# An attention and two feed-forward layers on one core: inverse sums per pair of heads, early signs on other engines, and a re-timed plan

## The chip, the cores and the metric

One core of a Trainium2 chip runs the whole program in one launch. The metric is the device time in microseconds (us) of one execution, as a median over runs; less is better. Engines are called PE (TensorE, matmuls), PEld (its weight loads), DVE (VectorE), ACT (ScalarE), POOL (GpSimd) and SP (SyncE, which issues the transfers).

## The reference

```python
def _attn_ref(q, k, v, proj):            # q, k, v: (2, 8, 768, 64); proj: (64, 6)
    q_bits = (einsum('bhsd,dk->bhsk', q, proj) > 0)
    k_bits = (einsum('bhsd,dk->bhsk', k, proj) > 0)
    mask = q_bucket[:, :, :, None] == k_bucket[:, :, None, :]   # buckets: the 6 bits as a number
    scores = where(mask, q @ k.T / 8, -1e9)
    attn = exp(scores - max(scores))
    attn = attn / (sum(attn) + 1e-09)
    return attn @ v

x = attn_out as (1536, 512)
h = x @ w_in;  x = (h * sigmoid(h)) @ w_out            # 512 -> 2048 -> 512
a, b = x @ w1, x @ w2                                  # 512 -> 1024 each
out = ((a * b) @ w3) @ w_out2                          # 1024 -> 1024 -> 512
```

All of it is float32. There are 16 heads, worked on as 8 pairs.

## The kernel before, in words

**Order of the work.** Nothing is written in the order in which it runs. The kernel hands many small operations to a planner (`Plan`), each with the engines that may run it and a length in ns for each, the operations that it waits for, the buffers that it takes and gives back, and a due time. `Plan.run` (L184) plays the program: it goes through the engines again and again, takes the one that can start earliest, and there the ready operation with the earliest due time, whose instructions it writes at once. The result is one fixed list per engine, and on the chip each engine works through its list in order: an instruction that waits holds up all behind it. Due times are shifted by a table `OFF` (L43 on) with one number per name of operation and stage of the program (`shift`, L112). So a length or a number of that table moves instructions between places and, where an operation may run on two engines, between engines. Lengths cost no time on the chip.

**Attention.** Per pair of heads q, k and the two heads' V are loaded (`fetch`, `fetch_v`), the hash bits are projected (L584) and compared (L590), and per head there are six units of 128 queries. A unit is one score pass on PE (L717; mask bits ride along as extra rows), the row maximum on DVE (`peak`, L733), the exponent on ACT (`exp`, L739, which also adds up its row sums), and a transposition of 32x32 blocks on DVE (`swap`, L757). Scores have two PSUM buffers, exponents two in SBUF. When all twelve units of a pair are transposed, six weighing passes on PE multiply them with V (`weigh`, L775), and ACT and DVE move the results out (`move`, L794 and L796). Pair 0 is `lone`: one score pass (L729) fills both buffers, for both heads of the pair.

V has one buffer. The next pair's V is loaded when the last weighing pass of the pair before has read it; two copies (`double`, a helper whose lines are L320 on ACT and L324 on POOL) put it on the upper 64 partitions too.

**Inverse sums.** For each head the sums [128 x 6] get a constant added (L804) and are inverted (L805) on DVE, turned on PE (`flip`, L808), copied to SBUF by ACT (`unload`), sent to DRAM by a transfer (`send`) and read back onto 64 partitions (`spread`); `norm` multiplies the pair's result with them.

**Weights.** They arrive as 64-bit words, 512 KB at a time, in half blocks of 512 columns, and become float32 in `piece`: ACT takes the high word (`high`, L366), ACT or POOL the low word (`low`, L370 or L374), DVE joins them (`join`, L380) and the sign is put in: in early weights (needed before 60.5 us: w_out2 and the first block of w3) by DVE (`sign`, L385), in those after it by ACT and POOL (`side`, L391, and `signed`, L394). Then a high and a low part for PE are made of each (`hi`, `lo`).

**Combine passes.** w3 and w_out2 are multiplied into one matrix beforehand (`product`, L852): 8 blocks of 8 groups of three matmuls of 512 columns, 192 in all, laid between the attention's passes. The block `it` may start when the weighing of a given pair is done.

**Feed-forward.** After the attention PE works through the two layers (L1014, L1132, L1176), 1920 matmuls of 512 columns; a few of them (blocks called early, and those on the first 512 tokens) already stand among pair 7's passes. Two token blocks are folded: sums and differences of them are made and split by ACT and DVE (`split_pair`), and seven products give what eight would (`rise_pair`, L1014).

## Time and profile before

| | |
|---|---|
| median of 3 runs | 730.82 us (730.27 to 735.04) |
| the profiled execution, its own time | 735.71 us |
| its span, first to last instruction | 733.9 us |
| busy: PE, DVE, ACT, POOL | 686.0, 566.3, 379.7, 288.2 us |
| mean granted clock of PE | 0.963 of full speed |

How to read it: the span is what the profile shows, the 1.8 us around it are start and end. Busy shares are means over stages that have different limits, so the rows below go by stretches. A granted clock of 1.00 is 2.4 GHz and 0.50 is 1.2 GHz; a mean between them says for how much of a stretch either was granted.

### The profile page before, as it was taken

The page shows a single profiled execution, that of the slowest core. Times are in us where ns is not written, and L with a number is a line of the kernel's source. Part 1 is how long each engine was busy: PE and PEld are TensorE (multiplying, and loading weights), DVE is VectorE, ACT ScalarE, POOL GpSimd, SP SyncE. Part 2 cuts the span into 40 slices and gives each one's busy share as a digit, 9 for nine tenths or more (in the row PEclk, how much of TensorE's full clock was granted, in tenths as well). Part 3 has the DMA queues.
Part 4 walks back from the last instruction along what each step waited for, and adds up shares of the span by engine and source line. Part 5 has one row for each costly group of instructions (what it writes and reads, how often), then busy time and mean ns, then how long its engine had stood idle before and what let it go on. Part 6 is the DMA issues. An engine that isn't in the chain of part 4 may idle for free.

```text
span 733.9 us, 14436 instructions
## 1 busy us (share of the span) xinstructions
PE 686.0 (93%) x5800; PEld 555.3 (76%) x5800; DVE 566.3 (77%) x829; ACT 379.7 (52%) x700; POOL 288.2 (39%) x274
## 2 busy tenths in 40 slices
PE   7877879989979898799999999999999999999997
PEld 5656667767757677687788888888888888888876
DVE  5888858877878799599899897977898826938255
ACT  4655747666674767555755454343554635323030
POOL 3744976885867732344124213022263220210000
PEclk8779699999998999999999999999999999999999
DMA  7534646455555432501231411112010211100004
GB/s 213 162 113 110 185 126 179 114 180 136 159 142 155 130 117 73 185 1 58 87 95 49 144 57 44 44 58 87 29 57 15 82 63 50 50 1 1 0 1 171
DMA packets 22882, 68.34 MB, mean 93 GB/s; under 512 B 3872, under 2 KB 4640, under 8 KB 22304
## 3 DMA queue, kind: packets, MB, share of 16 engines
q1 hardware_dynamic: 22816, 67.43, 30.3%
q8 instruction: 45, 0.74, 0.4%
q14 instruction: 21, 0.17, 0.1%
HBM read 55.58 MB, written 5.29 MB: 83 GB/s over the span
## 4 chain that ended last, share of the span: by engine, by line
PE 71%; DVE 9%; DMA 8%; ACT 6%; issue 4%; POOL 2%; SPq 0%; ACTq 0%; POOLq 0%; DVEq 0%
PE more L1176 18%; PE more L1014 13%; PE more L1132 6%; PE acc L1176 6%; PE acc L775 6%; PE score L717 6%; PE acc L1014 5%; PE acc L1132 4%; DMA V<-in_v 4%; ACT P L739 2%; PE turn L775 2%; PE score L729 2%; DMA raw<-in_w 2%; DVE y L327 1%; DMA raw<-in_wo 1%
## 5 line engine op out<-in xcount | busy, mean ns | idle before, releaser
L1014 PE MATMUL more<-y,piece 128*128 128x512 f32 x462 | 111.5, 390 | 1.6 <-ACT sg L320 0.7
L757 DVE STREAM_TRANSPOSE pt<-P 128x768 f32<-128x768 f32 x96 | 91.6, 966 | 20.9 <-ACT P L739 20.8
L739 ACT ACTIVATE P<-score,st 128x768 f32<-128x768 f32 x96 | 85.9, 896 | 40.2 <-DVE st L733 35.0
L733 DVE TENSOR_REDUCE st<-score 128x1 f32<-128x770 f32 x96 | 89.0, 944 | 22.1 <-PE score L717 16.6
L1014 PEld LDWEIGHTS more<-y,piece 128*128 128x128 f32 x462 | 86.4, 188 | 20.8 <-ACT sg L320 1.1
L1176 PE MATMUL more<-gh,piece 128*128 128x512 f32 x284 | 96.4, 389 | 0.0
L775 PE MATMUL turn<-pt,V 32*64 32x193 f32 x1536 | 77.2, 340 | 4.5 <-issue 4.3
L775 PE MATMUL acc<-pt,V 32*64 32x193 f32 x1536 | 77.4, 340 | 3.0 <-DVE x L1079 2.0
L1195 DVE SCALAR_TENSOR_TENSOR X<-more,X 128x512 f32<-128x512 f32 x93 | 62.6, 682 | 14.7 <-PE more L1176 14.5
L717 PE MATMUL score<-ka,qa 128*128 128x384 f32 x168 | 51.6, 390 | 23.3 <-ACT P L739 12.7
L775 PEld LDWEIGHTS acc<-pt,V 32*64 32x64 f32 x1536 | 60.7, 136 | 10.6 <-issue 6.6
L775 PEld LDWEIGHTS turn<-pt,V 32*64 32x64 f32 x1536 | 58.2, 136 | 7.9 <-issue 7.3
L1176 PEld LDWEIGHTS more<-gh,piece 128*128 128x128 f32 x284 | 53.2, 188 | 11.2 <-DVE piece L327 0.2
L717 PEld LDWEIGHTS score<-ka,qa 128*128 128x128 f32 x168 | 29.1, 202 | 42.2 <-ACT P L739 20.3
L1132 PE MATMUL more<-x,piece 128*128 128x512 f32 x240 | 59.1, 389 | 0.0
L1176 PE MATMUL more<-gl,piece 128*128 128x512 f32 x142 | 55.3, 389 | 0.0
L852 PE MATMUL acc<-piece,piece 128*128 128x512 f32 x192 | 52.1, 409 | 0.7 <-ACT X L794 0.7
L1132 PEld LDWEIGHTS more<-x,piece 128*128 128x128 f32 x240 | 45.0, 188 | 9.4
L374 POOL TENSOR_SCALAR t<-raw 128x512 uint32<-128x512 uint32 x22 | 15.7, 714 | 79.9 <-DMA raw<-in_wo 38.0
L717 PE MATMUL score<-kb,qb 76*128 76x384 f32 x168 | 45.6, 354 | 0.0
L1176 PE MATMUL more<-piece,gh 128*128 128x512 f32 x144 | 44.4, 389 | 0.0
L1014 PE MATMUL acc<-y,piece 128*128 128x512 f32 x168 | 43.1, 391 | 0.3 <-ACT sg L320 0.3
(192 smaller groups left out, 1461.0 us busy)
## 6 DMA issues: line engine op xcount, KB each, us to landing
raw<-in_w SPq DMA_DIRECT2D x24, 512.0 KB
raw<-in_wo SPq DMA_DIRECT2D x21, 512.0 KB
raw<-in_win SPq DMA_DIRECT2D x13, 512.0 KB
...
```

The lines of the kernel that those rows point to most:

```text
L374: engine[e].tensor_scalar(out=plan[t], in0=pair(raw)[:, :, 0], scalar1=0.875 * 2.0 ** -29, scalar2=0.49, op0=ALU.mult, op1=ALU.add,)
L717: nc.tensor.matmul(out=sc[:, g, :HF], lhsT=lhs[:k, qs], rhs=rhs[:k, g * HF:g * HF + HF], start=(k == 128), stop=(k != 128),)
L729: nc.tensor.matmul(out=plan["S", "u", side * NQ + i][:, g, :HF], lhsT=lhs[k, qs], rhs=rhs[k, g * HF:g * HF + HF], start=(p == 0), stop=(p ...
L733: nc.vector.tensor_reduce(out=plan[uk("st")][:, 0:1], in_=plan[uk("S")][:, :, :HF + 1], op=ALU.max, axis=AX.XY, negate=True)
L739: nc.scalar.activation(out=plan[uk("P")], in_=plan[uk("S")][:, :, :HF], func=AF.Exp, bias=s[:, 0:1], accum_out=plan[hk("sums")][:, i:i + 1],)
L757: nc.vector.transpose(plan[mine][:, :, 32 * i:32 * i + 32], plan[uk("P")].rearrange("p g (b i) -> p (g b) i", i=32))
L775: nc.tensor.matmul(out=to[a][64 * side:64 * side + 64, :GW + 1], lhsT=V[rows_, c, side], rhs=plan[key(f"pt{side}")][rows_, c, :GW + 1], st ...
L852: nc.tensor.matmul(out=plan[key + ("ps",)], lhsT=w[:, a, k], rhs=r[:, c], start=(k == 0 and n == 0), stop=(k == 7 and n == 2),)
L1014: nc.tensor.matmul(out=plan[bk[b]], lhsT=w[:, a], rhs=y, start=(opens and j == 0 and m == 0), stop=(j == 1 and m == 2), skip_group_check=True)
L1132: nc.tensor.matmul(out=plan[key], lhsT=w[:, a], rhs=x, start=(k == 0 and n == 0), stop=(k == 3 and n == 2))
L1176: nc.tensor.matmul(out=plan[key], lhsT=a, rhs=x, start=(f == 0 and n == 0), stop=(f == 1 and n == 2))
L1195: nc.vector.scalar_tensor_tensor(out=dst, in0=plan[key], scalar=by, in1=dst, op0=ALU.mult, op1=ALU.add)
```

## The change

- **Inverse sums per pair.** Both heads of a pair write their sums into one [128 x 12] tile. It is turned as it is, ACT adds the constant while it copies the [12 x 128] result to SBUF, DVE inverts it there in place, and one send carries both heads. The add on DVE and the per-head steps are gone.
- **Signs.** `by_pool` now holds for the early weights too.
- **Lengths.** The planner counts 1200 ns instead of 390 on top of a `lone` score pass, 80 ns more on each other score pass and 100 ns more on each weighing pass. An operation without instructions, `settled`, makes it take V as there 3 us after its loads have ended in its play.
- **Table.** Every number of `OFF` is another.

```diff
 OFF = {
-    "add": (0.0, 0.0, 78.9, -161.2, -8.9),
+    "add": (0.0, 0.0, -12.7, -284.8, 10.05),
...
-                by_pool = BEGIN + 50 < need and beside
+                by_pool = beside
...
+        settled = op({"": 3000.0}, lambda e: None, loadv[:2], t0)
...
-            loadv.append(op({"POOL": 1467, "ACT": 1510}, double, loadv[:2], t0 + 4 + f))
+            loadv.append(op({"POOL": 1467, "ACT": 1510}, double, [settled], t0 + 4 + f))
...
-                        accum_out=plan[hk("sums")][:, i:i + 1],
+                        accum_out=plan[key("sums")][:, par * NQ + i:par * NQ + i + 1],
...
-                    sc = both[i] = op({"PE": 390 + 8 * (PE_MORE + HF * PE_COL) if lone else 4 * (PE_MORE + HF * PE_COL)},
+                    sc = both[i] = op({"PE": 1200 + 8 * (PE_MORE + HF * PE_COL) if lone else 80 + 4 * (PE_MORE + HF * PE_COL)},
...
-                    xo = op({"PE": 180 + 2 * PART * (18 + 2 * (GW + 1) * PE_COL)}, weigh, [*evicted[0], *evicted[1], *loadv[2:], xo],
+                    xo = op({"PE": 280 + 2 * PART * (18 + 2 * (GW + 1) * PE_COL)}, weigh, [*evicted[0], *evicted[1], *loadv[2:], xo],
...
-            def invert(e, hk=hk):
-                s = plan[hk("sums")]
-                nc.vector.tensor_scalar_add(s[:, :NQ], s[:, :NQ], (S + 1e-9) * FLOOR)
-                nc.vector.reciprocal(out=s[:, NQ:], in_=s[:, :NQ])
...
-            iv = op({"DVE": 1020}, invert, exps, te + 3)
-            fl = op({"PE": 110}, flip, [iv], te + 4, [("R", hk("it"))], [hk("sums")])
-            un = op({"ACT": act(128)}, unload, [fl], te + 4.5, [("wsb", hk("invt"))], [hk("it")])
...
+            if par == 1:
+
+                def flip(e, key=key):
+                    nc.tensor.transpose(plan[key("it")][:2 * NQ, :128], plan[key("sums")], ident)
+
+                def unload(e, key=key):
+                    nc.scalar.activation(out=plan[key("invt")][:2 * NQ, :128], in_=plan[key("it")][:2 * NQ, :128], func=AF.Copy,
+                                         bias=(S + 1e-9) * FLOOR)
+
+                def invert(e, key=key):
+                    x = plan[key("invt")][:2 * NQ, :128]
+                    nc.vector.reciprocal(out=x, in_=x)
+
+                fl = op({"PE": 110}, flip, pair_exps, te + 3, [("R", key("it"))], [key("sums")])
+                un = op({"ACT": act(128)}, unload, [fl], te + 3.5, [("wsb", key("invt"))], [key("it")])
+                iv = op({"DVE": 850}, invert, [un], te + 4)
```

Three places of the new lists. First PE, where the first combine passes stand (L852 before, L857 now; `ka_113` and `ka_114` are the two heads' buffers). Before:

```order
L717 MATMUL score_80<-ka_114,qa_110 128x384 x2
L717 MATMUL score_80<-kb_116,qb_112 128x384 x2
L717 MATMUL score_79<-ka_113,qa_109 128x384 x2
L717 MATMUL score_79<-kb_115,qb_111 128x384 x2
L852 MATMUL acc_81<-piece_83,piece_87 128x512 x3
L717 MATMUL score_80<-ka_113,qa_109 128x384 x2
L717 MATMUL score_80<-kb_115,qb_111 128x384 x2
L852 MATMUL acc_81<-piece_83,piece_87 128x512 x3
L852 MATMUL acc_81<-piece_84,piece_87 128x512 x6
```

Now, on the same engine:

```order
L717 MATMUL score_80<-ka_114,qa_110 128x384 x2
L717 MATMUL score_80<-kb_116,qb_112 128x384 x2
L584 MATMUL turn_77<-qraw_103,pt 32x384 x2
L584 MATMUL turn_77<-kraw_104,pt 32x384 x2
L857 MATMUL acc_82<-piece_83,piece_87 128x512 x6
L857 MATMUL acc_82<-piece_84,piece_87 128x512 x6
L857 MATMUL acc_82<-piece_85,piece_87 128x512 x6
L717 MATMUL score_79<-ka_114,qa_110 128x384 x2
L717 MATMUL score_79<-kb_116,qb_112 128x384 x2
L857 MATMUL acc_82<-piece_86,piece_87 128x512 x3
```

Before, the first group stands behind the first scores of pair 2 (its first head, `ka_113`), one group at a time; now six groups in a row stand behind the tenth of its twelve score passes (second head, `ka_114`). Counted by pair, from its first score pass to the next pair's, the 64 groups stood as 16, 12, 15, 13 and 8 in pairs 2 to 6 and stand now as 10, 15, 13, 16 and 10.

Second DVE, where pair 0 ends and pair 1 begins (`P_117` and `P_118` are the exponents' buffers; `pt_125` and `pt_126` are pair 0's swapped tiles, `pt_127` is pair 1's first; L590 is the comparison of hash bits). Before:

```order
L733 TENSOR_REDUCE st_122<-score_80 128x1
L590 TENSOR_SCALAR bits_108<-turn_78,sel 128x384
L804 TENSOR_SCALAR sums_123<-sums_123 128x6
L805 RECIPROCAL sums_123<-sums_123 128x6
L733 TENSOR_REDUCE st_119<-score_79 128x1
L380 SCALAR_TENSOR_TENSOR acc_81<-acc_81,t_95 128x512
L733 TENSOR_REDUCE st_120<-score_80 128x1
L804 TENSOR_SCALAR sums_124<-sums_124 128x6
L805 RECIPROCAL sums_124<-sums_124 128x6
L385 SCALAR_TENSOR_TENSOR x_93<-raw_91,acc_81 128x512
L757 STREAM_TRANSPOSE pt_125<-P_117 128x24x32
L380 SCALAR_TENSOR_TENSOR acc_82<-acc_82,t_94 128x512
```

Now, on the same engine (L813 is the new reciprocal):

```order
L733 TENSOR_REDUCE st_122<-score_80 128x1
L380 SCALAR_TENSOR_TENSOR t_95<-acc_81,t_95 128x512
L757 STREAM_TRANSPOSE pt_125<-P_117 128x24x32
L757 STREAM_TRANSPOSE pt_126<-P_118 128x24x32
L733 TENSOR_REDUCE st_119<-score_79 128x1
L733 TENSOR_REDUCE st_120<-score_80 128x1
L813 RECIPROCAL wsb_96<-wsb_96 12x128
L757 STREAM_TRANSPOSE pt_127<-P_117 128x24x32
L733 TENSOR_REDUCE st_121<-score_79 128x1
```

The last swaps of pair 0 stood behind the first two maxima of pair 1 and both inversions; now they stand ahead of them, and the one reciprocal of the pair comes behind.

Third ACT, from the moves of a pair's weighed results to the copy of the next pair's V (`fv` is the move's added column, `wsb` the unloaded sums). Before:

```order
L794 ACTIVATE X<-acc_81,fv_106 128x6x32
L366 ACTIVATE acc_81<-raw_91 128x512
L320 ACTIVATE wsb_96<-turn_78 6x128
L739 ACTIVATE P_117,sums_124<-score_79,st_121 128x768
L366 ACTIVATE acc_81<-raw_90 128x512
L739 ACTIVATE P_118,sums_124<-score_80,st_122 128x768
L391 ACTIVATE x_93<-raw_91 128x512
L320 ACTIVATE wsb_96<-turn_78 6x128
L320 ACTIVATE V_105<-V_105 64x1536
```

Now, on the same engine:

```order
L794 ACTIVATE X<-acc_81,fv_106 128x6x32
L366 ACTIVATE acc_81<-raw_91 128x512
L739 ACTIVATE P_117,sums_123<-score_79,st_119 128x768
L366 ACTIVATE acc_81<-raw_90 128x512
L739 ACTIVATE P_118,sums_123<-score_80,st_120 128x768
L391 ACTIVATE x_93<-raw_91 128x512
L320 ACTIVATE x_97<-X 128x512
L739 ACTIVATE P_117,sums_123<-score_79,st_121 128x768
L320 ACTIVATE qa_110<-qraw_103 64x768
L391 ACTIVATE x_92<-raw_90 128x512
L739 ACTIVATE P_118,sums_123<-score_80,st_122 128x768
L320 ACTIVATE V_105<-V_105 64x1536
```

The copy of V stood two exponents behind the moves and stands now four behind them.

Elsewhere: eight `side` steps (L391) and seven `low` steps (L370) now stand among the exponents of pair 0 on ACT, where no `side` and one `low` stood. Between PE's last weighing pass and its first matmul on folded blocks stood 144 matmuls and stand now 120.

## Rows read from the trace of the kernel before

**Rows 1.** Stretches: pairs 0 to 6, pair 7, two after it. Length, busy, clock, DMA.

```profile
core 0: us, PE busy (x) PEld busy (x) DVE busy (x) ACT busy (x) POOL busy (x), PEclk, DMA share, GB/s
9.00:44.40 35.40, 30.05 (x169) 20.42 (x169) 27.96 (x36) 20.55 (x36) 21.89 (x21) 0.72 0.55 174
44.40:76.60 32.20, 22.34 (x443) 18.11 (x441) 27.79 (x40) 19.49 (x41) 15.80 (x14) 0.87 0.42 119
76.60:119.90 43.30, 37.98 (x494) 30.39 (x494) 31.38 (x42) 26.64 (x53) 31.07 (x29) 0.85 0.54 151
119.90:150.90 31.00, 28.26 (x478) 22.95 (x478) 25.54 (x34) 20.64 (x43) 26.65 (x23) 1.00 0.54 150
150.90:184.50 33.60, 31.34 (x487) 24.30 (x487) 26.29 (x35) 23.10 (x46) 23.51 (x21) 1.00 0.55 154
184.50:218.80 34.30, 29.61 (x481) 23.11 (x481) 27.68 (x36) 22.11 (x44) 25.63 (x22) 1.00 0.53 149
218.80:251.40 32.60, 28.94 (x469) 23.44 (x469) 26.14 (x34) 20.42 (x40) 25.30 (x23) 0.90 0.50 141
251.40:302.70 51.30, 46.83 (x888) 38.78 (x888) 43.48 (x64) 31.70 (x64) 15.15 (x14) 0.97 0.40 120
302.70:342.00 39.30, 37.26 (x158) 30.63 (x159) 35.03 (x53) 20.86 (x40) 17.80 (x15) 0.96 0.13 41
342.00:733.90 391.90, 386.24 (x1698) 317.79 (x1696) 291.04 (x446) 171.19 (x301) 84.52 (x89) 1.00 0.17 58
```

**Rows 2.** The combine passes alone (L852) in pairs 2 to 6; columns PE and PEld.

```profile
76.60:119.90 43.30, 14.41 (x48) 10.51 (x48) 0.85 0.54 151
119.90:150.90 31.00, 9.22 (x36) 6.64 (x36) 1.00 0.54 150
150.90:184.50 33.60, 11.73 (x45) 8.29 (x45) 1.00 0.55 154
184.50:218.80 34.30, 10.38 (x39) 7.17 (x39) 1.00 0.53 149
218.80:251.40 32.60, 6.34 (x24) 4.33 (x24) 0.90 0.50 141
```

**Rows 3.** Groups by line: count, busy us, mean ns, idle before and its releaser.

```profile
L757 DVE STREAM_TRANSPOSE pt<-P 128x768 f32<-128x768 f32 x96 | 91.6, 966 | 20.9 <-ACT P L739 20.8
L733 DVE TENSOR_REDUCE st<-score 128x1 f32<-128x770 f32 x96 | 89.0, 944 | 22.1 <-PE score L717 16.6 <-PE score L729 4.9
...
L739 ACT ACTIVATE P<-score,st 128x768 f32<-128x768 f32 x96 | 85.9, 896 | 40.2 <-DVE st L733 35.0 <-DVE pt L757 3.9 <-PE turn L775 0.8
...
L394 POOL TENSOR_TENSOR x<-t,x 128x512 f32<-128x512 f32 x18 | 22.9, 1281 | 4.0 <-ACT x L391 3.5
...
L366 ACT ACTIVATE acc<-raw 128x512 f32<-128x512 f32 x28 | 17.6, 627 | 4.0 <-DMA raw<-in_w 2.4 <-DVE x L385 1.2 <-PE acc L526 0.2
...
L320 ACT ACTIVATE V<-V 64x1536 f32<-64x1536 f32 x9 | 13.3, 1486 | 4.7 <-DMA V<-in_v 4.6
...
L391 ACT ACTIVATE x<-raw 128x512 f32<-128x512 f32 x18 | 11.7, 660 | 0.0
...
L804 DVE TENSOR_SCALAR sums<-sums 128x6 f32<-128x6 f32 x16 | 9.9, 621 | 0.0
...
L385 DVE SCALAR_TENSOR_TENSOR x<-raw,acc 128x512 uint32<-128x512 uint32 x10 | 6.7, 666 | 0.1
...
L796 DVE TENSOR_SCALAR X<-turn,fv 128x192 f32<-128x192 f32 x16 | 5.9, 413 | 0.3
```

**Rows 4.** The add of the sums by itself, and the reciprocal's group by line.

```profile
L804 DVE TENSOR_SCALAR sums<-sums x16: 127/172/1733, 44.6 to 288.3; 128x6 f32<-128x6 f32 x16
...
L805 DVE RECIPROCAL sums<-sums 128x6 f32<-128x6 f32 x16 | 3.1, 191 | 0.6
```

**Rows 5.** PE in order of time, near 51 us: start, us, engine, line.

```profile
50.95 0.44 PE L717 MATMUL score<-ka,qa 128*128 128x384 f32 x1 [2.20 <-ACT P L739]
```

**Rows 6.** Waits of ACT and POOL for V: us in all, times, longest.

```profile
POOL V L324 <- DMA V<-in_v: 10.7, 7, 2.9
ACT V L320 <- DMA V<-in_v: 4.6, 5, 1.4
```

More of the change, by code (lines that the diff above doesn't have):

```diff
@@ new lines @@
+    "again": (0.0, 0.0, -160.35, 0.0, 0.0),
+    "aside": (0.0, 0.0, 0.0, 0.0, 23.2),
+    "begin": (0.0, 155.1, -102.15, 0.0, -65.25),
+    "double": (22.15, 30.85, 56.7, 0.0, 0.0),
+    "exp": (-83.65, -32.35, 130.8, 0.0, 0.0),
+    "fall": (0.0, -156.25, -23.35, 11.55, -43.25),
+    "fetch": (-12.15, 118.85, 0.0, 0.0, 0.0),
+    "fetch_v": (-30.7, 66.05, 0.0, 0.0, 0.0),
+    "flip": (67.0, 22.1, 35.5, 0.0, 0.0),
+    "fold": (0.0, 0.0, -46.7, 0.0, -38.75),
+    "g_hi": (0.0, -13.3, 3.85, 40.95, 114.9),
@@ new lines @@
+    "left": (-4.65, 91.5, 0.0, 0.0, 0.0),
+    "lend": (0.0, 74.95, 0.0, 0.0, 0.0),
+    "lo": (-92.8, -191.1, -309.8, -94.7, -99.45),
+    "lo_sum": (0.0, 0.0, 80.1, -5.0, 44.65),
+    "load": (69.45, 46.6, 46.35, -15.9, 64.75),
+    "low": (-79.95, 114.55, 127.15, 66.4, 53.95),
+    "mark_k": (-5.1, 0.0, 0.0, 0.0, 0.0),
+    "marks": (-175.05, -109.6, 98.4, 0.0, 0.0),
+    "meet": (0.0, 0.0, 0.0, 0.0, -159.5),
+    "more_": (0.0, 0.0, -22.35, 33.5, 234.1),
+    "move": (-104.0, -115.25, 2.25, 0.0, 0.0),
@@ new lines @@
+    "round_": (-22.1, 0.0, 0.0, 0.0, 0.0),
+    "scores": (-47.15, -15.7, -17.8, 0.0, 0.0),
+    "scores_lone": (-204.0, 0.0, 0.0, 0.0, 0.0),
+    "send": (-139.1, -69.85, -115.3, 0.0, 0.0),
+    "settle": (0.0, -24.7, 0.0, 0.0, 0.0),
+    "setup": (-151.0, 0.0, 0.0, 0.0, 0.0),
+    "side": (-37.15, 182.35, 0.0, 0.0, 0.0),
+    "sign": (161.45, 47.05, 254.5, 94.85, 282.35),
+    "signed": (-61.85, -37.95, 0.0, 0.0, 0.0),
+    "snap": (0.0, 0.0, -14.95, -13.3, -5.0),
+    "spread": (-47.95, 38.85, 30.85, 0.0, 0.0),
@@ L109 @@
+    "squash": (0.0, -22.1, -3.7, -9.8, 12.0),
+    "swap": (-17.35, 56.4, 153.0, 0.0, 0.0),
+    "total": (0.0, 0.0, -155.4, -126.3, 15.95),
+    "unload": (-44.6, -53.95, 153.5, 0.0, 0.0),
+    "warm": (0.0, -187.25, 0.0, 0.0, 0.0),
+    "weigh": (1.3, -2.7, -80.8, 0.0, 0.0),
+    "weight": (-64.7, -23.95, 0.0, 0.0, 0.0),
+    "x_hi": (0.0, 148.35, 130.6, 0.0, -76.95),
+    "x_lo": (0.0, 86.95, -56.2, 0.0, -245.55),
 }
@@ L697, in lsh_attention_moe_kernel @@
                  give=[] if lone else [key("qraw"), key("kraw"), key("bits")])
-        both, evicted, moves, spreads = {}, {}, [], []
+        both, evicted, moves, spreads, pair_exps = {}, {}, [], [], []
         for par in range(2):
```

112 lines of the change are left out of this document (34 added, 78 removed).

## The prediction

> **What bounds the kernel now.** Read the page first: busy shares by engine, the 40 slices, the granted clock. It shows two halves: from about 300 us TensorE is busy nearly without a break, before that no engine is. So the second view is the table of stretches, cut where the first scores of each pair of heads start [rows 1]. It gives one row per pair (0 to 7; the last row of the attention also holds pair 7's weighing), and the reader is to see three things.
>
> From 342 us on TensorE is busy 386.24 of 391.9 us at clock 1.00, with 1698 matmuls, that is 0.2275 us each. No edit changes their number, so nothing is to be had there. From 302.7 to 342 VectorE is busy 35.03 of 39.3 us beside TensorE's 37.26: a place that could become tight.
>
> In the attention a pair takes 31.0 to 34.3 us when all goes well (pairs 3 to 6). Pair 2 takes 43.3 us and pair 1 takes 32.2 us though it has hardly any work for TensorE (22.34 us busy). Both stand at a mean clock of 0.87 and 0.85. Pair 2's row is long because TensorE is busy 37.98 us in it: 48 matmuls of the combine pass (w3 times w_out) cost 14.41 us there, 0.30 each, against 0.256 in pair 3 at clock 1.00 (9.22 by 36) [rows 2]. Beside that it is idle 5.3 us.
>
> VectorE's floor per pair follows from the groups by line [rows 3]: 12 maxima of 944 ns and 12 swaps of 966 ns are 22.9 us. With moves, joins and inverses it stands at 25.5 to 31.4 us [rows 1]. So a pair cannot fall much below 27 us, and pairs with combine passes are held by TensorE and VectorE together.
>
> **The change part by part.** Inverse sums. Gone are 16 adds (L804, mean 621 ns, for the wait inside them can be long: 127 ns at the least, 1733 at the most) and 16 reciprocals of 6 columns (191 ns) [rows 3, 4]: 1.62 us of VectorE per pair. In their place stands one reciprocal of 128 columns on 12 partitions. The trace has none. It cannot be cheaper than 0.19 us, the same instruction on 6 columns, nor dearer than 128/6 of it, 4.07 us. I take 1.5: the row of 6 columns lies 64 ns above the cheapest add of the same 6, 10.7 ns a column, so 127 ns + 128 x 10.7. So VectorE's load is the same within 0.1 us a pair; between the ends it is -1.4 to +2.5. In pairs 3 to 6 it hides under TensorE (28.3 to 31.3 us busy); if that cover were gone, the dear end would cost up to 2.5 us in pairs 1 and 2 each. Eight sends, flips and unloads fall away, the spreads stay 16. Term: 0, from -2 to +5.
>
> The Trainium skill, "VectorE: DVE Perf Modes" (First, the fixed hardware budget), says that a reciprocal repeats its divide step 8 times, so a column would cost 8 beats at 0.96 GHz: 1.07 us for 128 columns, 1.2 with the 127 ns, an estimate from that page. By it the term would still be 0.
>
> Signs of the early weights. Ten L385 instructions of 666 ns leave VectorE (6.7 us); ten `side` of 660 ns come to ScalarE and ten `signed` of 1281 ns to GpSimd [rows 3]. In the order of ScalarE eight `side` and six more `low` of about the size of `high` (627 ns) come into pair 0: 9.0 us onto 20.55 of 35.4 us. That looks covered. But pair 0 is a ring: both score buffers are filled by one pass, so scores, maxima and exps follow each other six times, 5.9 us a turn, with two exps (2 x 0.90 [rows 3]) in it: 4.1 us are left between them. After the change one such gap holds a V copy of 1486 ns and five half-block steps of about 0.64 each: 4.7 us, 0.6 late. The first turn has a `side` between its two exps, 0.66 late. Others fit. GpSimd's 21.89 us have room for 10 us more. Term: +1, from -1 to +3.
>
> Pair 1. Before, VectorE's list puts two joins, two signs, two inverses and two maxima ahead of swaps whose exps are long done; TensorE waits 2.20 us for an exp that waits for these swaps [rows 5]. After, the swaps come first, and only one reciprocal stands ahead of a swap. VectorE's sum is then 22.9 + 0.83 (two moves, 413 ns) + 1.5 + 1.3 (two joins, taken as long as a sign) = 26.6 us [rows 3]; I put pair 1 at 27. Term: -5, from -6 to -1.
>
> Pair 2. In TensorE's order the first combine pass came behind the first scores of pair 2 and comes now behind its tenth: up to pair 3's first scores 10 groups of three stand there, where 16 were. 18 of 48 matmuls leave, 14.41 x 18/48 = 5.4 us, and since the rest come at the end, the waits for their weight pieces go too. Pair 3 took 31.0 us with 36 of them at full clock; I put pair 2, with 30, at 34, three more for its lower clock. Term: -9, from -13 to -3.
>
> The groups that left: pairs 3 to 6 get 15, 13, 16 and 10 groups for 12, 15, 13 and 8 [rows 2]: +9, -6, +9 and +6 matmuls, 18 x 0.256 = 4.6 us. TensorE's idle time there is 2.7, 2.3, 4.7 and 3.7 us [rows 1], enough by number, but it lies in waits for exps that need not move. I take some two thirds as seen: +3, from 0 to +5.
>
> V copies. Planned 3 us later, they stand behind four exps after the moves, where they stood behind two. ScalarE waited 4.6 us in five of them, GpSimd 10.7 in seven [rows 6]; an exp stands behind each of ScalarE's. Pairs 1 and 2 already hold part of that. V is used half a pair later, so a later copy costs nothing as long as it is not moved behind the first weighing. Term: -1, from -5 to +1.
>
> After the attention. Between the last weighing and the first pass on folded blocks stood 144 matmuls, and now 120: 24 x 0.2275 = 5.5 us less time for VectorE to fold and split [rows 1]. Its row leaves 4.3 us of idle time. Term: +1, from -2 to +6.
>
> Sum: 0 + 1 - 5 - 9 + 3 - 1 + 1 = -10 us. The profiled execution, 735.71 us, would be 725.7. It lies 4.9 us above the median shown, 730.82; off that median the same sum gives 721.
>
> **The rivals.** The clock. Without combine passes TensorE is idle more in pair 2, and a clock that falls there would take back more than is gained. Pair 3's work without them is 28.26 - 9.22 = 19.0 us at full clock [rows 1, 2], 38 us at half. Pairs 1 and 2 would then take 38 each plus 30 matmuls at twice 0.256 (15.4): 91.4 us for 75.5, +15.9; with the +3 of the moved groups +19, so 750. It decides where the mean granted clock of these pairs falls below 19.0/29 = 0.66. Against it: pair 1 had no combine pass before and stood at 0.87.
>
> The Trainium skill, "TensorE: Matmul & The Clock Gate" (HAM oscillation), says that idle gaps between bursts bring the engine back to half rate and each next burst begins cold. The rows agree so far as clocks of 0.72 to 0.87 stand where idle time is largest; by the rule alone, this rival would be likelier than I make it.
>
> The work only moves. If pair 2 was long for its waits on loads and V and not for the combine passes, it gives 3 us; pair 1 gives 4, the moved groups cost their 4.6 and the other terms +1: -1.4, so 729. For it: TensorE's 5.3 us of idle time in pair 2. Against: 14.41 us at 0.30 a matmul.
>
> All idle time is used. Pair 2 at 30 us (-13), the moved groups free, the rest as in the sum: -17, so 714. For it: the idle sums above.
>
> **How the numbers follow.** Forecast 721, chance 0.50, its own range 715 to 728. Work only moves, 729: 0.27. All idle time used, 714: 0.15. Clock, 750: 0.08. About 1% (7.3 us) is what a measurement of this kernel can tell from no change. Faster by more than that, under 723.5: the whole of 714, some three quarters of the forecast's share, together 0.54. Slower, above 738: the clock and a scrap, 0.09. Within: 0.37. The range that leaves 2 in 10 out reaches from 710 to 736: below, the terms' favourable ends of pair 2 and the V copies; above, the work that only moves with 6 us more after the attention.
>
> **What would show it.** Right: pair 1 near 27 us, pair 2 near 34 with 30 combine matmuls, pairs 3 to 6 between 31 and 36, the last weighing about 11 us earlier than 302.7, the stretch behind it 431 to 433 us, a reciprocal of 1 to 2 us, pair 0 within 34 to 38. Wrong: clocks under 0.66 in pairs 1 and 2 (the clock), pair 2 over 39 (work only moves), exps of pair 0 waiting for loads or joins, or matmuls on folded blocks waiting for VectorE.

## The result and the profile after

| | before | after |
|---|---|---|
| median, 4 runs each | 730.67 us (730.27 to 735.04) | 722.63 us (721.02 to 724.97) |
| the profiled execution | 735.71 us | 722.41 us |
| busy: PE, DVE, ACT, POOL | 686.0, 566.3, 379.7, 288.2 us | 680.8, 548.8, 395.8, 276.7 us |

The ratio is 0.9879 with a 95% interval of 0.9833 to 0.9925: 8 us less by the medians, where 10 were forecast. The two profiled executions lie 13.3 us apart, since that of before is 5 us above its median. So the lengths by pair below add up to some 13 us and not to 8.

The stretches of the kernel after, each cut where a pair's first scores start:

```profile
core 0: us, PE busy (x) PEld busy (x) DVE busy (x) ACT busy (x) POOL busy (x), PEclk, DMA share, GB/s
8.50:44.10 35.60, 27.22 (x179) 18.76 (x178) 29.02 (x37) 29.20 (x52) 28.72 (x26) 0.86 0.65 200
44.10:70.20 26.10, 21.39 (x433) 16.63 (x434) 24.48 (x32) 18.41 (x39) 17.90 (x16) 0.89 0.46 127
70.20:101.70 31.50, 30.04 (x471) 23.95 (x472) 26.40 (x34) 22.41 (x43) 23.91 (x20) 0.88 0.53 144
101.70:135.00 33.30, 31.11 (x488) 24.10 (x486) 25.35 (x34) 23.92 (x47) 25.32 (x22) 1.00 0.56 152
135.00:171.00 36.00, 33.55 (x481) 25.48 (x482) 25.31 (x33) 23.81 (x45) 23.22 (x21) 0.86 0.52 147
171.00:205.60 34.60, 32.11 (x490) 24.69 (x489) 26.05 (x34) 24.32 (x45) 27.35 (x25) 1.00 0.57 160
205.60:242.00 36.40, 33.02 (x497) 26.17 (x496) 26.41 (x35) 25.21 (x48) 28.28 (x25) 1.00 0.56 164
242.00:293.00 51.00, 43.17 (x867) 35.36 (x865) 42.65 (x59) 30.12 (x60) 12.02 (x10) 0.93 0.35 104
293.00:332.20 39.20, 38.71 (x163) 31.59 (x164) 37.00 (x56) 25.67 (x47) 17.70 (x14) 0.96 0.17 55
332.20:720.60 388.40, 383.89 (x1693) 317.21 (x1691) 282.46 (x444) 169.73 (x297) 71.35 (x85) 1.00 0.17 57
```

They answer to [rows 1], with one correction. The cut at 76.60 us there was one unit early: TensorE still worked on pair 1's last scores at 76.7 us, and pair 2's first scores started at 78.2. With the right cuts pairs 1 and 2 of the kernel before read:

```profile
44.50:78.20 33.70, 23.70 (x447) 19.47 (x446) 29.06 (x43) 20.77 (x43) 17.23 (x15) 0.85 0.41 120
78.20:120.00 41.80, 36.52 (x491) 28.95 (x490) 30.06 (x42) 25.35 (x50) 29.73 (x27) 0.87 0.55 152
```

So where did the time go? Lengths in us between the starts of the first scores, after minus before: pair 0 +0.1, pair 1 -7.6, pair 2 -10.3, pairs 3 to 6 +2.3, +2.4, +0.4 and +3.7, pair 7 -0.2, all behind the last weighing -3.5. The reader is to see in the rows that pair 1 fell to VectorE's floor (24.48 us busy of 26.10, with 32 instructions where 43 stood), that pair 2 fell most, and that pairs 3 to 6 gave back 8.8 of the 17.9 us that pairs 1 and 2 gained.

The combine passes alone (L857 now) in pairs 2 and 3 of the kernel after, which answer to [rows 2]:

```profile
70.20:101.70 31.50, 7.33 (x30) 5.54 (x30) 0.88 0.53 144
101.70:135.00 33.30, 11.88 (x46) 8.18 (x45) 1.00 0.56 152
```

Three groups by line of the kernel after (columns as in [rows 3]):

```profile
L757 DVE STREAM_TRANSPOSE pt<-P 128x768 f32<-128x768 f32 x96 | 90.5, 958 | 5.8 <-ACT P L739 5.7
L733 DVE TENSOR_REDUCE st<-score 128x1 f32<-128x770 f32 x96 | 89.0, 941 | 33.8 <-PE score L717 31.2 <-PE score L729 2.1
...
L813 DVE RECIPROCAL wsb<-wsb 12x128 f32<-12x128 f32 x8 | 7.4, 920 | 0.0
```

The new reciprocal takes 0.92 us. VectorE waits less for exps before its swaps (5.8 us, 20.9 in [rows 3]) and more for scores before its maxima (33.8, where it was 22.1). That second number is where the give-back in pairs 3 to 6 stands: by the rows above VectorE has 2.5 us less to do in these four pairs and is idle 11.3 us more. It leads to what follows.

**A row of weighing passes.** In pair 2 the kernel before does the weighing of pair 1. Its VectorE there, in order of time (start, us, engine, line, what; in brackets the idle time before it and what ended it):

```profile
99.70 1.54 DVE L804 TENSOR_SCALAR sums<-sums 128x6 f32<-128x6 f32 x1
101.27 0.19 DVE L805 RECIPROCAL sums<-sums 128x6 f32<-128x6 f32 x1
107.79 0.96 DVE L733 TENSOR_REDUCE st<-score 128x1 f32<-128x770 f32 x1 [6.33 <-PE score L717]
110.18 0.96 DVE L733 TENSOR_REDUCE st<-score 128x1 f32<-128x770 f32 x1 [1.44 <-PE score L717]
```

And its TensorE, with the rows of L775 left out:

```profile
96.76 0.52 PE L717 MATMUL score<-kb,qb 76*128 76x384 f32 x2
...
106.70 0.62 PE L717 MATMUL score<-ka,qa 128*128 128x384 f32 x2
```

Between these two score passes stand 256 matmuls of L775, by the stretch alone with L775:

```profile
97.30:106.60 9.30, 7.44 (x256) 6.88 (x256) 0.82 0.53 160
```

A weighing pass is 64 matmuls, so these are four of a pair's six in a row. For 9.3 us no scores come, both score buffers are soon used up, and VectorE, which has 25 to 30 us of work in a pair, stands for 6.33 us. In the kernel after the same weighing goes as 1, 2, 1 and 2 passes with scores between them, and VectorE's longest wait in pair 2 is the copy at the head of a move:

```profile
87.14 1.79 DVE L733 TENSOR_REDUCE st<-score 128x1 f32<-128x770 f32 x2
90.98 0.16 DVE L322 COPY fv<-turn 128x1 f32<-128x1 f32 x1 [2.05 <-PE turn L775]
91.98 1.83 DVE L733 TENSOR_REDUCE st<-score 128x1 f32<-128x770 f32 x2
```

In pairs 4 to 6 it is the other way round: the longest row was 2, 2 and 3 passes before and is 3 in each after, and VectorE waits there once or twice for 3.2 to 5.6 us in every pair.

### The profile page after: what moved, and what is told of

It is laid out like the page before. It is cut to its first block, busy times and chain, and to the rows that moved or that the text cites. A ratio compares the mean times of both kernels' runs of the same rounds, so it can differ in the third digit from the quotient of the medians.

```text
span 720.6 us, 14384 instructions
## 1 busy us (share of the span) xinstructions
PE 680.8 (94%) x5792; PEld 549.1 (76%) x5792; DVE 548.8 (76%) x799; ACT 395.8 (55%) x717; POOL 276.7 (38%) x265
## 4 chain that ended last, share of the span: by engine, by line
PE 73%; DVE 9%; ACT 5%; issue 4%; DMA 4%; POOL 3%; SPq 0%; DVEq 0%; ACTq 0%; POOLq 0%
PE more L1181 18%; PE more L1019 14%; PE more L1137 8%; PE acc L775 7%; PE acc L1181 7%; PE score L717 5%; PE acc L1019 5%; PE turn L775 3%; PE acc L1137 2%; DVE pt L757 2%; ACT P L739 2%; PE acc L857 2%; DVE st L733 2%; DVE y L327 2%; DMA kraw<-in_kT 1%
## 5 line engine op out<-in xcount | busy, mean ns | idle before, releaser
L1019 PE MATMUL more<-y,piece 128*128 128x512 f32 x474 | 117.6, 389 | 0.7 <-ACT qraw L320 0.7
L733 DVE TENSOR_REDUCE st<-score 128x1 f32<-128x770 f32 x96 | 89.0, 941 | 33.8 <-PE score L717 31.2
L1019 PEld LDWEIGHTS more<-y,piece 128*128 128x128 f32 x474 | 88.9, 188 | 19.6 <-ACT qraw L320 1.2
L739 ACT ACTIVATE P<-score,st 128x768 f32<-128x768 f32 x96 | 85.8, 895 | 28.7 <-DVE st L733 18.4
L1181 PE MATMUL more<-gh,piece 128*128 128x512 f32 x268 | 91.7, 390 | 0.1
L775 PE MATMUL turn<-pt,V 32*64 32x193 f32 x1536 | 78.4, 344 | 8.9 <-issue 8.8
L775 PE MATMUL acc<-pt,V 32*64 32x193 f32 x1536 | 77.9, 344 | 1.4 <-issue 0.8
L1200 DVE SCALAR_TENSOR_TENSOR X<-more,X 128x512 f32<-128x512 f32 x88 | 59.5, 685 | 23.7 <-PE more L1181 23.0
L775 PEld LDWEIGHTS acc<-pt,V 32*64 32x64 f32 x1536 | 60.5, 139 | 10.8 <-issue 7.5
L775 PEld LDWEIGHTS turn<-pt,V 32*64 32x64 f32 x1536 | 58.0, 138 | 12.0 <-issue 11.7
L717 PE MATMUL score<-ka,qa 128*128 128x384 f32 x168 | 51.7, 390 | 12.7 <-ACT P L739 11.3
L1137 PE MATMUL more<-x,piece 128*128 128x512 f32 x264 | 62.9, 389 | 0.0
L1181 PEld LDWEIGHTS more<-gh,piece 128*128 128x128 f32 x268 | 50.3, 188 | 10.9 <-DVE X L1200 0.5
L1137 PEld LDWEIGHTS more<-x,piece 128*128 128x128 f32 x264 | 49.6, 188 | 10.3
L717 PEld LDWEIGHTS score<-ka,qa 128*128 128x128 f32 x168 | 28.7, 201 | 33.4 <-ACT P L739 23.8
L1181 PE MATMUL more<-gl,piece 128*128 128x512 f32 x134 | 52.2, 389 | 0.0
L857 PE MATMUL acc<-piece,piece 128*128 128x512 f32 x192 | 50.3, 397 | 1.4 <-ACT X L794 1.4
L374 POOL TENSOR_SCALAR t<-raw 128x512 uint32<-128x512 uint32 x15 | 10.8, 717 | 100.9 <-DVE x L385 28.9
L370 ACT ACTIVATE t<-raw 128x512 uint32<-128x512 uint32 x46 | 30.8, 670 | 32.9 <-DMA raw<-in_w 21.1
L1181 PE MATMUL more<-piece,gh 128*128 128x512 f32 x144 | 44.3, 389 | 0.0
```

Source lines behind the costliest of these rows:

```text
L370: nc.scalar.activation(out=plan[t], in_=pair(raw)[:, :, 0], func=AF.Copy, scale=0.875 * 2.0 ** -29, bias=0.49)
L717: nc.tensor.matmul(out=sc[:, g, :HF], lhsT=lhs[:k, qs], rhs=rhs[:k, g * HF:g * HF + HF], start=(k == 128), stop=(k != 128),)
L733: nc.vector.tensor_reduce(out=plan[uk("st")][:, 0:1], in_=plan[uk("S")][:, :, :HF + 1], op=ALU.max, axis=AX.XY, negate=True)
L739: nc.scalar.activation(out=plan[uk("P")], in_=plan[uk("S")][:, :, :HF], func=AF.Exp, bias=s[:, 0:1], accum_out=plan[key("sums")][:, par * ...
L775: nc.tensor.matmul(out=to[a][64 * side:64 * side + 64, :GW + 1], lhsT=V[rows_, c, side], rhs=plan[key(f"pt{side}")][rows_, c, :GW + 1], st ...
L857: nc.tensor.matmul(out=plan[key + ("ps",)], lhsT=w[:, a, k], rhs=r[:, c], start=(k == 0 and n == 0), stop=(k == 7 and n == 2),)
```

## The experiments

Two kinds of kernel stand below. Where an edit "keeps the order", the planner still plays the program of the changed kernel, and only the instruction itself is another. Otherwise the planner runs anew, and every list can come out differently. "Before" was measured beside each set of four (medians 734.21, 732.81 and 733.05 us), so ratios are what compares between sets. The expectations number their theories anew in each set.

**1. The combine passes early again.** The changed kernel, with two numbers of the table put back:

```diff
-    "product": (59.65, 97.45, 0.0, 0.0, 0.0),
+    "product": (12.85, 59.65, 0.0, 0.0, 0.0),
```

> The changed kernel with the kernel before's numbers for the combine passes alone (OFF of product), so that 16 groups of three stand in pair 2 again, not 10. Theory 1 (the gain came from the order of the work: combine passes out of pair 2): pair 2 grows from 31.5 to 35 us or more, the time goes up by 2 to 6 us, to 725 to 729. Theory 2 (it came from work taken off VectorE: inverse sums and signs): no change, 721 to 724.

Measured: 725.75 us (719.73 to 727.24), ratio 0.9871 (0.9807 to 0.9935), no different from the change itself. The interval is wide (5 us to either side), so the reading rests on the trace. Its combine passes in pairs 2 and 3:

```profile
73.70:109.90 36.20, 11.42 (x48) 8.85 (x48) 0.89 0.48 133
109.90:138.60 28.70, 6.99 (x28) 4.97 (x27) 1.00 0.60 169
```

With all 48 matmuls back pair 2 takes 36.2 us (31.5 with 30 of them) and pair 3 takes 28.7 (33.3): 4.7 us up, 4.6 down. Pair 2 grew as theory 1 said, and the time did not. So moving combine passes moves time and gains none. The plan was made anew, and VectorE's work moved with them (29.55 us in pair 2 where the kernel after has 26.40), so the price is that of a group with all that hangs on it. Pair 2 as a whole, and VectorE's longest wait in it:

```profile
73.70:109.90 36.20, 34.36 (x490) 27.27 (x491) 29.55 (x38) 27.69 (x52) 28.86 (x24) 0.89 0.48 133
```

```profile
94.29 0.16 DVE L322 COPY fv<-turn 128x1 f32<-128x1 f32 x1 [1.83 <-PE turn L775]
```

This divides pair 2's 10.3 us: 4.7 go with the combine passes that left, and 5.6 with something else, for with 48 matmuls, as many as before, the pair is still that much shorter than 41.8 us. Two things differ. The row of four weighing passes is gone in this kernel too (1, 2, 1, 2), and it held VectorE for 6.33 us. And the combine passes stand behind the tenth score pass here as well and not at the head of the pair: the 48 cost 11.42 us, where they cost 14.41 before, since a quarter of them stood at half clock there. L852 in the kernel before, in that stretch alone and by line over the whole span (busy, mean ns, idle time before and what ended it):

```profile
78.20:85.90 7.70, 4.86 (x11) 3.94 (x12) 0.50 0.81 190
...
L852 PE MATMUL acc<-piece,piece 128*128 128x512 f32 x192 | 52.1, 409 | 0.7 <-ACT X L794 0.7
```

No run separates the two. VectorE's rows speak for the first: its idle time in the pair fell from 11.7 to 6.7 us and its longest wait from 6.33 to 1.83 us, while up to 90 us, beside those dear matmuls, it had waited 2.3 us in all.

**2. Three reciprocals for one.** Order kept; the two added ones write to a spare tile.

```diff
+                    for _ in range(2):
+                        nc.vector.reciprocal(out=spare[:2 * NQ, :128], in_=x)
```

> The changed kernel, same order on every engine, each pair's reciprocal issued three times (two go to a spare tile): 16 more instructions of 0.92 us, 14.7 us more of VectorE, which is more than the change took off it by the inverses. Theory 1: hidden but for pairs 1 and 2, 0 to +3 us, 722 to 726. Theory 2: VectorE's load sets the pairs' length, +7 to +13 us, 730 to 735.

Measured: 734.92 us (731.91 to 736.42), ratio 1.0003 (0.9969 to 1.0036), some 9 us above the change. The two rows of the reciprocals:

```profile
L815 DVE RECIPROCAL spare<-wsb 12x128 f32<-12x128 f32 x16 | 14.9, 931 | 0.3
L816 DVE RECIPROCAL wsb<-wsb 12x128 f32<-12x128 f32 x8 | 7.5, 941 | 0.3
```

14.9 us more of VectorE cost 9 us, and pairs 1 to 6 are each longer, by 0.9 to 3.5 us. So in this list VectorE's time is not covered by TensorE's.

**3. The early signs by VectorE, in the places of the new list.** Order kept: ten signs of the early weights stand on VectorE again, and ScalarE's and GpSimd's instructions for them are left out.

```diff
+                early = BEGIN + 50 >= need
+                def side(e, raw=raw, x=x, t=t, early=early):
+                    if early:
+                        nc.vector.scalar_tensor_tensor(
...
+                            op0=ALU.bitwise_and, op1=ALU.bitwise_or,
```

> The changed kernel, same order, the ten early signs put in by VectorE again at the place where ScalarE's step stood: VectorE +6.7 us, ScalarE -6.6, GpSimd -12.8, nearly all in pairs 0 and 1. Theory 1: -2 to +2 us, 720 to 725. Theory 2: +3 to +6 us, 726 to 729.

Measured: 729.41 us (727.24 to 733.90), ratio 0.9952 (0.9920 to 0.9984), 4 to 5 us above the change. Pairs 0 and 1 of this kernel:

```profile
8.10:47.70 39.60, 29.18 (x179) 20.25 (x178) 34.70 (x44) 25.74 (x44) 20.31 (x20) 0.81 0.51 167
47.70:77.50 29.80, 23.41 (x433) 18.61 (x434) 27.35 (x35) 17.21 (x36) 13.11 (x11) 0.79 0.44 128
```

VectorE has 5.7 us more to do in pair 0 and 2.9 in pair 1, and these pairs are 4.0 and 3.7 us longer; pairs 4 and 7 are 1.6 and 2.1 us shorter. Both stand close to VectorE's floor: it is idle 4.9 and 2.5 us of them. But the ten signs are dearer here than they were (666 ns each in the kernel before, [rows 3]), so the run overstates what leaving them out is worth:

```profile
L400 DVE SCALAR_TENSOR_TENSOR x<-raw,t 128x512 uint32<-128x512 uint32 x10 | 10.7, 1069 | 0.0
```

**4. q and k loaded earlier.** The chain of waits of the kernel after holds two loads that the kernel before did not have there:

```profile
142.94 5.24 DMA kraw<-in_kT
179.75 5.55 DMA kraw<-in_kT
```

```diff
-    "fetch": (-12.15, 118.85, 0.0, 0.0, 0.0),
+    "fetch": (-12.15, 60, 0.0, 0.0, 0.0),
```

> The changed kernel with one number of the table less (fetch, from 118.85 to 60), which puts the load of k straight behind that of q in SyncE's list in all pairs; before, sends and spreads of the inverse sums stood between them in pairs 4 to 6. If the late k (landing 5.2 us after its issue, ScalarE waiting behind it, then 10 us at half clock in pair 4) costs what its row shows: pair 4 from 36.0 to 33 us, and 717 to 720 in all. Rival: another wait ends at the same place, 721 to 724.

Measured: 725.61 us (723.15 to 729.43), ratio 0.9897 (0.9839 to 0.9956): no gain. Pair 4 took 34.8 us (36.0 in the kernel after, 37.0 in run 5), not the 33 expected. As far as one plan made anew can tell, the loads on the chain were not what the time hung on.

**5. The changed kernel again, beside the next three.**

> The changed kernel itself, on this chip, as the mark for the runs beside it. Both theories: 0.983 to 0.993 of the kernel before.

Measured: 725.02 us (721.54 to 726.89), ratio 0.9891 (0.9849 to 0.9933). Its pairs lie within 0.8 us of those of the first profile in pairs 0 to 3 and 6, and up to 2.6 above it in pairs 4 and 5: so much a single pair varies with the same lists, and a difference of that size in one pair alone says nothing.

**6. The inverse on 12 columns.** Order kept but for the inverse itself, which stands at the place of the turning: ScalarE adds the constant on [128 x 12] (0.21 us), VectorE inverts there, and then the tile is turned.

```diff
+                    s = plan[key("sums")]
+                    nc.scalar.activation(out=s, in_=s, func=AF.Copy, bias=(S + 1e-9) * FLOOR)
+                    nc.vector.reciprocal(out=s, in_=s)
...
-                    nc.vector.reciprocal(out=x, in_=x)
```

> The changed kernel, same order, the constant added by ScalarE and the reciprocal made on the [128 x 12] sums before they are turned: about 0.25 us of VectorE per pair for 0.92, 5.4 us less in all, 0.2 us more of ScalarE per pair. Theory A (each us of VectorE in the attention counts nearly in full, since maxima, exps and swaps follow each other in a ring): 3 to 6 us faster than the changed kernel. Theory B (what counts is where the plan puts the work; the three reciprocals hurt only by the place they stood at): -1 to +1 us.

Measured: 727.0 us (720.62 to 729.51), ratio 0.9905 (0.9873 to 0.9937): no gain. Three groups by line:

```profile
L757 DVE STREAM_TRANSPOSE pt<-P 128x768 f32<-128x768 f32 x96 | 91.2, 964 | 12.1 <-ACT P L739 11.8
...
L807 DVE RECIPROCAL sums<-sums 128x12 f32<-128x12 f32 x8 | 1.8, 227 | 1.6 <-ACT sums L806 1.6
...
L808 PE MATMUL turn<-ident,sums 128*12 128x128 f32 x8 | 2.4, 301 | 7.4 <-DVE sums L807 7.4
```

The reciprocal fell from 7.4 to 1.8 us in all, and VectorE waits 12.1 us before its swaps where it waited 5.8: what was saved came back as waiting for exps. So taking time off VectorE did not help by itself here. But the edit is not a clean test of that: the turning now waits for the reciprocal, and TensorE stood 7.4 us before it, where it stood 0.5 in the kernel after. What a shorter reciprocal at the old place would give is not shown.

**7. The kernel before with the inverse per pair alone**, and **8. with the early signs alone**; planned anew with the old table and lengths. Of the first edit, which is the change's whole part on inverse sums, two lines stand here; the second is one line.

```diff
-                        accum_out=plan[hk("sums")][:, i:i + 1],
+                        accum_out=plan[key("sums")][:, par * NQ + i:par * NQ + i + 1],
...
+                fl = op({"PE": 110}, flip, pair_exps, te + 3, [("R", key("it"))], [key("sums")])
```

```diff
-                by_pool = BEGIN + 50 < need and beside
+                by_pool = beside
```

> The kernel before with the inverse sums per pair alone, table, lengths and signs as they were. VectorE: 0.92 us per pair for 1.62, -5.6 us. Theory A: 3 to 6 us faster than the kernel before. Theory B: the plan is redone, -2 to +2 us, and the pairs' lengths change by more than VectorE's sum.

> The kernel before with the early signs by ScalarE and GpSimd alone. VectorE -6.7 us in pairs 0 to 2. Theory A: 3 to 5 us faster than the kernel before, in pairs 0 and 1. Theory B: -2 to +2 us.

Measured: 747.71 us (743.28 to 750.60), ratio 1.0193 (1.0145 to 1.0241), and 734.87 us (732.62 to 737.11), ratio 1.0028 (1.0004 to 1.0052). Neither edit of the code makes the kernel faster under the old plan, and the inverse makes it 15 us slower, which is outside both theories. VectorE in the kernel with the inverse alone, all its waits of over 5 us from 60 to 320 us:

```profile
111.11 0.96 DVE L732 TENSOR_REDUCE st<-score 128x1 f32<-128x770 f32 x1 [6.28 <-PE score L716]
179.08 0.96 DVE L732 TENSOR_REDUCE st<-score 128x1 f32<-128x770 f32 x1 [5.91 <-PE score L716]
218.64 0.96 DVE L732 TENSOR_REDUCE st<-score 128x1 f32<-128x770 f32 x1 [7.55 <-PE score L716]
253.28 0.96 DVE L732 TENSOR_REDUCE st<-score 128x1 f32<-128x770 f32 x1 [5.65 <-PE score L716]
```

At each of them TensorE does four weighing passes in a row, in pairs 2, 4, 5 and 6, where the kernel before had such a row in pair 2 alone (and one in pair 7).

**9 to 12. Which part of the plan carries it.** The changed kernel, planned anew with one part undone: both edits of the code (9), the table (10), `settled` (11), the lengths of score and weighing passes (12).

```diff
-        settled = op({"": 3000.0}, lambda e: None, loadv[:2], t0)
+        settled = op({"": 0.0}, lambda e: None, loadv[:2], t0)
```

```diff
-                    sc = both[i] = op({"PE": 1200 + 8 * (PE_MORE + HF * PE_COL) if lone else 80 + 4 * (PE_MORE + HF * PE_COL)},
+                    sc = both[i] = op({"PE": 390 + 8 * (PE_MORE + HF * PE_COL) if lone else 4 * (PE_MORE + HF * PE_COL)},
...
-                    xo = op({"PE": 280 + 2 * PART * (18 + 2 * (GW + 1) * PE_COL)}, weigh, [*evicted[0], *evicted[1], *loadv[2:], xo],
+                    xo = op({"PE": 180 + 2 * PART * (18 + 2 * (GW + 1) * PE_COL)}, weigh, [*evicted[0], *evicted[1], *loadv[2:], xo],
```

> The changed kernel with both code edits undone (inversion per head on VectorE, early signs by VectorE) and with the new table, the new lengths and settled kept; the plan is made anew from them. Theory A, the table, the lengths and the code fit each other and none of them carries the gain: 729 to 745 us, a ratio to the kernel before of 0.998 or more. Theory B, the new numbers of the plan carry it, whatever the code is: 720 to 727 us, a ratio below 0.993.

> The changed kernel with the table OFF of the kernel before; code, lengths and settled are the new ones. Theory A, table and code fit each other: 729 to 750 us (the inverse alone under the old plan cost 15 us, the signs 2). Theory B in this form, that lengths and settled carry the gain and the table does not: 720 to 727 us.

> The changed kernel with a length of 0 for settled, so V's copies are planned right behind their loads again, and the plan made anew. Theory A, any number that is changed under a fitted table costs some of the fit: 724 to 735 us. Theory B, settled carries a good part of the gain by itself: 727 us or more together with V copies that wait 10 us or more for V on GpSimd and ScalarE, as they did in the kernel before. If settled does nothing: 721 to 726.

> The changed kernel with the old lengths of the score and weighing passes in the planner (390, 0 and 180 ns), settled kept, and the plan made anew. Theory A, the table is fitted to the lengths: 724 to 740 us, a time lost in pairs that the edit has no reason to touch. Theory B, the lengths do nothing by themselves: 721 to 726.

| | median, us | ratio to before (95%) |
|---|---|---|
| 9, both edits of the code undone | 772.57 (770.46 to 777.49) | 1.0542 (1.0495 to 1.0588) |
| 10, old table | 743.26 (741.64 to 747.95) | 1.0146 (1.0102 to 1.0190) |
| 11, `settled` at 0 | 749.69 (748.54 to 753.52) | 1.0243 (1.0196 to 1.0290) |
| 12, old lengths | 735.43 (729.38 to 739.83) | 1.0035 (1.0005 to 1.0065) |

Each part that is undone loses the whole gain and, but for the lengths, over 1% more. That is what the first theory forecast, with losses larger than it said in 9 and 11: table, lengths and code fit each other. Of the parts, only the two edits of the code (7 and 8) and the plan as a whole (9) were tried alone, and none of these carries the gain; the table, `settled` or the lengths alone in the kernel before were not run.

The reader is to see how a plan goes wrong. VectorE in kernel 9, in pair 4, and the copy's group by line over the whole span:

```profile
178.96 0.69 DVE L380 SCALAR_TENSOR_TENSOR t<-acc,t 128x512 uint32<-128x512 uint32 x1 [0.69 <-ACT acc L366]
192.43 0.16 DVE L322 COPY fv<-turn 128x1 f32<-128x1 f32 x1 [12.78 <-PE turn L776]
193.28 0.97 DVE L758 STREAM_TRANSPOSE pt<-P 128x768 f32<-128x768 f32 x1
```

```profile
L322 DVE COPY fv<-turn 128x1 f32<-128x1 f32 x8 | 1.3, 158 | 51.1 <-PE turn L776 51.1
```

All six weighing passes stand in a row there (384 matmuls in the stretch from 178.5 to 193 us), in VectorE's list the move stands next, and swaps whose exps are long done wait behind it: ScalarE's last two exps had ended at 169.0 and 170.7 us. The swaps account for a part of the wait only. Two exps and two maxima were ready, so four swaps, 3.9 us, could have gone first (an estimate from 966 ns each); for the rest VectorE had no scores to work on. That happens in pairs 1, 4, 5 and 6, for 9.87, 12.78, 12.94 and 12.44 us: 48 us of VectorE, of the 51.1 in the group, in a kernel whose span is 50 us longer than that of the change. In kernel 11 the same stands in pairs 2, 3 and 5 (12.05, 13.10 and 8.16 us; its span is 27 us longer), by its waits:

```profile
DVE fv L322 <- PE turn L775: 40.5, 6, 13.1
...
POOL V L324 <- DMA V<-in_v: 11.9, 5, 3.1
```

The waits for V came back with `settled` at 0, as the second theory said of them, but they are 11.9 us on GpSimd and 1.6 on ScalarE, beside 40.5 on VectorE. Kernel 10 has a row of six in pair 4 and rows of four in pairs 2, 5 and 6; VectorE's waits at the first two:

```profile
102.39 0.96 DVE L733 TENSOR_REDUCE st<-score 128x1 f32<-128x770 f32 x1 [5.54 <-PE score L717]
179.15 0.16 DVE L322 COPY fv<-turn 128x1 f32<-128x1 f32 x1 [11.13 <-PE turn L775]
```

The longest row of weighing passes in each pair, counted in TensorE's order of time, and the pair's length in us:

| kernel | pair 2 | pair 3 | pair 4 | pair 5 | pair 6 |
|---|---|---|---|---|---|
| before | 4: 41.8 | 2: 31.0 | 2: 33.6 | 2: 34.3 | 3: 32.6 |
| after | 2: 31.5 | 2: 33.3 | 3: 36.0 | 3: 34.6 | 3: 36.4 |
| 7 | 4: 44.3 | 3: 30.5 | 4: 38.6 | 4: 39.0 | 4: 34.6 |
| 8 | 4: 40.4 | 2: 31.4 | 2: 33.2 | 2: 34.1 | 3: 32.2 |
| 9 | 2: 33.9 | 2: 35.6 | 6: 47.4 | 6: 44.4 | 6: 45.6 |
| 10 | 4: 38.9 | 3: 32.2 | 6: 40.3 | 4: 38.3 | 4: 36.5 |
| 11 | 6: 40.0 | 6: 41.5 | 4: 36.1 | 6: 38.2 | 3: 33.3 |
| 12 | 2: 36.9 | 3: 35.9 | 3: 40.5 | 4: 35.5 | 2: 34.1 |

With two passes at most in a row a pair took 33.6 us on the mean (12 pairs), with three 34.4 (10), with four 38.5 (11), with six 42.5 (7). The groups differ in other things too: the pairs with rows of four and six hold 44 and 42 combine matmuls on the mean, those with two and three 36 and 34 (some 2 us at 0.24 to 0.26 us each), and their mean granted clock is 0.91 and 0.86, against 0.94 and 0.93. What the rows show in each case is VectorE standing while TensorE weighs: 5.5 to 7.8 us at the rows of four in the table, 8 to 13 us at a row of six. That fits the losses of kernels 7, 9, 10 and 11, and in pair 2 what the combine passes do not account for. No run joins or splits a row of passes and leaves all else as it was, so its price is read from traces and argued, not shown by an edit of its own.

It does not explain kernel 12. In pair 4 of it VectorE waits twice for scores:

```profile
165.54 0.96 DVE L733 TENSOR_REDUCE st<-score 128x1 f32<-128x770 f32 x1 [3.15 <-PE score L717]
173.93 0.96 DVE L733 TENSOR_REDUCE st<-score 128x1 f32<-128x770 f32 x1 [7.43 <-PE score L717]
```

The second wait is two passes with a gap of 2.48 us in them that the profile only calls "issue" (the last section says what goes with such gaps):

```profile
168.70 0.48 PE L775 MATMUL acc<-pt,V 32*64 32x193 f32 x3 [2.48 <-issue]
```

And pair 2, 36.9 us long with 27 combine matmuls, stands at a mean clock of 0.73, where pair 2 of the kernel after stands at 0.88:

```profile
70.70:107.70 37.00, 33.98 (x469) 26.07 (x470) 27.61 (x35) 22.36 (x45) 28.90 (x25) 0.73 0.44 122
```

Why the planner lays the passes in a row in one plan and apart in another stays open. Due times, lengths and the buffers' states in its play decide it together, and no run takes them apart.

## Why the prediction was right, and where not

The forecast of 721 us for 722.63 holds, as do its sign, its range and the places that it names first, pairs 1 and 2. By its steps:

- **Inverse sums, 0.** Right. The reciprocal was taken as 1.5 us and measures 0.92, which makes VectorE's load 0.7 us a pair less. Run 6 took away 0.69 us more a pair and gained nothing, though it made TensorE wait at the turning. But the cover named for a dear end was wrong: "in pairs 3 to 6 it hides under TensorE". In run 2 two more reciprocals a pair cost 9 us, and pairs 3 to 6 were longer by 0.9 to 3.5 us each, 8.7 in all. The Trainium skill, "VectorE: DVE Perf Modes" (First, the fixed hardware budget), by which the estimate was 1.07 to 1.2 us, came nearer than the extrapolated row; the measured 0.92 us lies below both.
- **Early signs, +1.** The sum for ScalarE was right (29.20 us busy in pair 0 where 29.6 were worked out) and pair 0 kept its length, 35.5 and 35.6 us. The +1 did not come. The step counted what the signs cost on ScalarE and left out what their absence saves on VectorE, though it named the 6.7 us that leave it. Run 3, which puts them back in the new list, is 4 to 5 us slower (4.0 us in pair 0 and 3.7 in pair 1, less what later pairs give back), but with 10.7 us of signs and not 6.7. Under the old plan, run 8, leaving them out costs 2 us (0.3 to 3.8). So the term has no sign of its own; it hangs on the list.
- **Pair 1, -5.** Right in its reason and short in its size: 26.1 us where 27 were forecast, with VectorE busy 24.48 of them. Measured against the right cut, 33.7, that is -7.6: VectorE has 4.6 us less to do there and is idle 3.0 us less. The cut one unit early had made pair 1 look 1.5 us shorter and pair 2 as much longer than they were.
- **Pair 2, -9.** The size was near (-10.3 us), and half of the step failed. "18 of 48 matmuls leave, 5.4 us" came near: run 1 puts them at 4.7 us, and at 4.6 in pair 3, where that run takes them away. The rest of the -9 was laid to "the waits for their weight pieces", and there were none: in the kernel before TensorE waited 0.7 us before its combine matmuls over the whole span, and for ScalarE (the row of L852 under run 1). What remains to be accounted for, 5.6 us, fits the row of four weighing passes that was split, with its wait of 6.33 us, and in part the matmuls that left the half clock. I had read pair 2's TensorE busy time and not the order of what stood in it, though the trace showed that wait.
- **The moved groups, +3.** Pairs 3 to 6 are 8.8 us longer, by +2.3, +2.4, +0.4 and +3.7. Pair 3's part is its 9 added matmuls at the price of run 1 (4.6 us for 18), so the idle time that was to hide a third of them hid nothing. The rest is not the groups: pair 4 has 6 matmuls fewer and is longer all the same. Pair 4 has the clock as well: it stands at 0.86, where it stood at 1.00 before, and in runs 3 and 6, whose lists differ only in the instruction tried, it stood at 1.00 and took 34.4 and 34.0 us, near the 33.6 of the kernel before. The clock is not all of it, for in run 5 pair 4 took 37.0 us at 0.95. In pairs 5 and 6, at full clock and with rows of three passes, VectorE's waits of 3.2 to 5.2 us are what the rows show.
- **V copies, -1.** The waits for V left the lists of ScalarE and GpSimd ([rows 6]: 4.6 and 10.7 us). Run 11 brought them back and lost 25 us, but VectorE's waits at weighings were three times as long as those for V. So `settled` acts by the order that it makes; what V's waits cost by themselves is not separated.
- **After the attention, +1.** It came out as -3.5 us (431.2 to 427.7). VectorE's load did get denser there, 37.00 of 39.2 us where 35.03 of 39.3 stood, and TensorE waited less all the same: idle 0.5 us of that stretch, 2.0 before. The time lost by VectorE that the step feared is not in the rows. The gain is not clear either: with the lists of the kernel after, runs 2, 3, 5 and 6 took 427.9 to 431.9 us here, and the kernel before was traced once.

Of the rivals, the clock did not come where it was forecast: pairs 1 and 2 stand at 0.89 and 0.88. It fell in pair 4 instead, from 146.3 us on, behind a wait of TensorE of 1.09 us for an exp. "The work only moves" was right about the combine passes, its object, and wrong about the total, since pair 2 got shorter for another reason than either case had. "All idle time is used" came near in pair 2 (31.5 us for its 30), and its moved groups were not free. That the sum came within 2 us of the result is luck in part, since errors cancel: the pairs 3 to 6 lost 6 us more than forecast, and pairs 1 and 2 and the end gained 8 more.

The larger lesson is in runs 7 to 12. The prediction took the change apart into edits with a price each. By the runs the edits have no such prices: under the old plan leaving the signs off VectorE costs 2 us and the inverse per pair 15, and the new plan without both is 40 us slower than the kernel before. The forecast's terms for pairs 1 and 2 were read from the two lists and not from the edits; that they held, and the term of the signs did not, agrees with this.
